# A fused decay attention and ELU layer on one core: one list of pieces in place of a plan that is worked out

## The chip, the core and the metric

One of the eight cores of a Trainium2 chip runs the whole kernel. The metric is the time of one execution in microseconds, the median of the runs shown.

## The reference

Attention with a decay per head runs over 4 batches, 8 heads, 768 positions and 64 columns a head. Its result, seen as 3072 tokens of 512 columns, goes through a layer of two matrices with an ELU between them. The reference goes in blocks of 64 positions; the arithmetic is this:

```python
intra = np.einsum('bhic,bhjc->bhij', qb, kb) * Dmask[None]      # Dmask = lam**(i-j) for i >= j
intra = np.einsum('bhij,bhjd->bhid', intra, vb)
inter = np.einsum('bhid,bhde->bhie', qb * lam_pow[None], kv_state)
out[:, :, sl] = intra + inter
kv_state = lam_block[None, :, None, None] * kv_state + np.einsum('bhsd,bhse->bhde', kb * rev_pow, vb)
...
x = out.transpose(0, 2, 1, 3).reshape(3072, 512)
h = x @ w_in                                                     # 512 x 2048
g = np.where(h > 0.0, h, np.exp(np.minimum(h, 0.0)) - 1.0)
return g @ w_out                                                 # 2048 x 512
```

## The kernel before

The work is cut into 24 blocks of 128 positions, all 8 heads together. Block g belongs to batch g % 4 and to place g // 4 in its sequence, so a block needs the state that block g - 4 left. Both kernels name the steps of a block by letters:

- L: GpSimd issues the loads of q, k and v, which turn float32 into float16 on the way. The first four blocks are loaded alone (128 KB as float16), the others in pairs (256 KB). q of block 0 comes as float32 through SP (`raw_q`) and is cast on DVE. The weights come through the same GpSimd queue in eight slices each, `wi16_0` to `wi16_7` and `wo16_0` to `wo16_7` (wi0, wo0 and so on below, 256 KB each).
- T: q and k are transposed, for blocks 0 to 7 by eight TensorE transposes (`att_T_pe`, L273) with an evacuation of q on DVE (L280, which also scales it by `qs`) and one of k on ACT (L281), for blocks 8 to 23 by two DMA transposes on SP's queue (`att_T_dma`, L258).
- S: the scores, eight matmuls into two PSUM banks (L292); two DVE instructions multiply them by the decay mask (`pp`, L308).
- P: the masked scores times v, and from block 4 on the state times q (L328, L334). One evacuation makes the block's columns of x, `xt` (ACT L349 up to block 7, DVE L351 after).
- U: the block's own part of the state (L387 for one block, L396 for a pair). It reads `kd`, the decayed k that GpSimd makes (L164), and is added on DVE (L408) to the old state that GpSimd has decayed (`stt`, L368, called M).
- the first product of the layer (L468): one piece fills one PSUM bank `psH` of two. For blocks 0 to 3 a piece is four column tiles of one block, 16 matmuls of 128 columns; from block 4 on it is two column tiles of a pair, 8 matmuls of 256 columns. Then ACT makes the exponential (`e`, L474) and the relu (L475), and DVE joins them into `g` (L447), called G in what follows. The piece is named 1:0:0 before and A0:0 after (first block, number).
- the second product (L489): four matmuls of 512 columns into the block's bank `psM`, four such pieces for a block. It is named 2:0:0 before and B0:0 after. Piece j reads wo slices 2j and 2j+1. After the last piece ACT copies the bank out (L515) and SP stores 256 KB. The last 128 columns of block 23 are made by 16 small matmuls at the end (L501).

Each engine runs its instructions in the order in which the program lists them. Before, that order comes from three sources. `POOL_ORDER` is GpSimd's own list up to the loads of block 10. `OPEN` is a list by hand, up to the second product of block 6. After it a loop puts one first product of a pair after another and between them what `AT` says (loads 18 pieces ahead, the DMA transposes 13 ahead, S 8 ahead, P and U together 4 ahead), with one second product after each first one. DVE's work of S, P and U is not put down where TensorE's is: it goes into the list `late`, of which `flush` takes one entry after each G. A store is issued when the next output is ready (`emit_stores(1)`). `BANKS` gives the PSUM banks: T0, T1 and T2 have one bank for q and one for k, the later T one for both.

```python
        if late:
            late.pop(0)()
...
        prog.append(f"1:{g}:{j}")
        prog += extra.pop(u, [])
        n = 2
        while m2 and need[m2[0]] <= u - 2 and n and len(m2) - (len(m1) - 1 - x) > LAGU:
            prog.append("2:%d:%d" % m2.pop(0))
            n -= 1
```

Of the kernel before, what the change touches and what calls it, by code (L numbers as in the profile page):

```python
# [11 lines left out]
ALU = mybir.AluOpType  # L12


@with_exitstack
def kernel(
# [11 lines left out]
    nc = tc.nc  # L28
# [5 lines left out]
    DFF = moe_w_in.shape[1]  # L34
    NFT = DFF // 128
# [3 lines left out]
    NJ = NFT // FB  # L39
    GPE = 8  # L40
    LAST = NG - 1
    CUT = 384
    GSIZE = {**{g: 1 for g in range(4)}, **{g: 2 for g in range(4, NG, 2)}}
    GFIRST = {g0 + i: g0 for g0, n in GSIZE.items() for i in range(n)}
    WI = [2] * 8
    WO = [2] * 8
    POOL_ORDER = (
        "k0 k1 iota q1 k2 v1 i0 v0 q2 i1 v2 i2 o0 i3 d0 q3 o1 i4 k3 i5 o2 o3 v3 d1 m4 d2 d3 i7 "
        "o4 o5 i6 o7 k4 o6 q4 m5 k6 v4 q6 k10 q10 d5 d4 d6 m6 v6 k8 q8 v8 d7 m7 v10"
    )  # L50
    RAW = "q0"
    FIRST = "q0:0 c0 c1 c2"
    OPEN = (
# [7 lines left out]
    )  # L61
    LAGU = 7
    AT = {"L": -18, "W": -13, "T": -9, "S": -8, "B": -4}
    BANKS = (
        "S0=M0,M1 S1=C,D S2=D,M1 S3=D,B P0=M1 P1=B P2=B P3=D U0=M0 U1=D U2=A U3=M1 T0=M1,C "
        "T1=D,A T2=A,D T3=D T4=M0 T5=A T6=M1 T7=D M2=C M3=M0"
    )
    TAGS = {w: t.replace(",", " ") for w, t in (x.split("=") for x in BANKS.split())}

# [4 lines left out]
    asb = ctx.enter_context(tc.tile_pool(name="asb", bufs=1))  # L74
    msb = ctx.enter_context(tc.tile_pool(name="msb", bufs=1))
    ps = ctx.enter_context(tc.tile_pool(name="ps", bufs=1, space=bass.MemoryType.PSUM))

    lam_b = cpool.tile([128, H], FP32, name="lam_b")
    nc.sync.dma_start(out=lam_b[:], in_=lam.unsqueeze(0).broadcast_to([128, H]))

    GROUPS = [(0, 1), (1, 1), (2, 1), (3, 1)] + [(i, 2) for i in range(4, NG, 2)]
    size_of = dict(GROUPS)
    group_of = {g + i: (g, i) for g, n in GROUPS for i in range(n)}
    st = [
        [cpool.tile([128, NHP, 128], FP16, name=f"st{b}_{i}") for i in range(2)]
        for b in range(B)
    ]
    qg, kg, vg = {}, {}, {}  # L90

    def emit_load(w, g0):
        n = size_of[g0]
        c, b = divmod(g0, B)
        x = {"q": q, "k": k, "v": v}[w]
        src = x[b : b + n, :, c * L : (c + 1) * L].rearrange("b h p d -> p (b h) d")
        t = asb.tile([128, n, H, 64], FP16, tag=f"{w}n{n}", name=f"{w}n{g0}", bufs=4)
        {"q": qg, "k": kg, "v": vg}[w][g0] = t
        nc.gpsimd.dma_start(out=t[:].rearrange("p b h d -> p (b h) d"), in_=src)  # L99


    raw = {}
    for w in RAW.split():
        x = {"q": q, "k": k}[w[0]]
        g0 = int(w[1:])
        raw[w] = asb.tile([128, H, 64], FP32, name=f"raw_{w}", tag=f"raw_{w}")
        (nc.sync if w[0] == "q" else nc.scalar).dma_start(
            out=raw[w][:], in_=x[g0, :, 0:L].rearrange("h p d -> p h d")
        )
    nc.scalar.preload_act_table_set("natural_log_exp_and_others")  # L110

    def cast_raw(g, w, eng):
        n = f"{w}{g}"
        t = asb.tile([128, 1, H, 64], FP16, tag=f"{w}n1", name=f"{w}n{g}", bufs=4)
        (qg if w == "q" else kg)[g] = t
        if eng == 0:
            nc.vector.tensor_copy(t[:, 0], raw[n][:])  # L117
        else:
            nc.scalar.copy(t[:, 0], raw[n][:])

    def of(tiles, g):
        g0, i = group_of[g]
        return tiles[g0][:, i]

    wi16, wo16, wi_of, wo_of = [], [], {}, {}
    for i, w in enumerate(WI):
        wi16.append(wpool.tile([128, NHP, w * 128], FP16, name=f"wi16_{i}", tag=f"wi16_{i}"))
        for j in range(w):
            wi_of[sum(WI[:i]) + j] = (i, j)
    for i, w in enumerate(WO):  # L130
        wo16.append(wpool.tile([128, w, DM], FP16, name=f"wo16_{i}", tag=f"wo16_{i}"))
        for j in range(w):
            wo_of[sum(WO[:i]) + j] = (i, j)
    assert sum(WI) == NFT and sum(WO) == NFT

    def emit_wi(i):
        f0 = sum(WI[:i]) * 128
        nc.gpsimd.dma_start(  # L138
            out=wi16[i][:],
            in_=moe_w_in[:, f0 : f0 + WI[i] * 128].rearrange("(k p) f -> p k f", p=128),  # L140
        )

    def emit_wo(i):
        f0 = sum(WO[:i]) * 128
        nc.gpsimd.dma_start(
            out=wo16[i][:],
            in_=moe_w_out[f0 : f0 + WO[i] * 128, :].rearrange("(n p) f -> p n f", p=128),
        )

    iota_c = cpool.tile([128, 1], I32, name="iota_c")  # L150
    iota_r = cpool.tile([128, 128], I32, name="iota_r")

    def emit_iota():
        nc.gpsimd.iota(iota_c[:], pattern=[[0, 1]], base=0, channel_multiplier=1)
        nc.gpsimd.iota(iota_r[:], pattern=[[1, 128]], base=0, channel_multiplier=0)

    kds, qkT, Pt, psS, xg = {}, {}, {}, {}, {}

    def att_kd(g):
        if g // B == NCB - 1:  # L160
            return
        kd = asb.tile([128, H, 64], FP16, tag="kd", name=f"kd{g}", bufs=8)
        kds[g] = kd
        nc.gpsimd.tensor_tensor(  # L164
            out=kd[:], in0=of(kg, g),
            in1=ks[:].unsqueeze(2).broadcast_to([128, H, 64]), op=ALU.mult,
        )


    pool_list = POOL_ORDER.split()  # L170

    def emit_pool():
        w = pool_list.pop(0)
        if w == "iota":
# [75 lines left out]
    for g in range(NG):  # L250
        default_tags(g)
# [401 lines left out]
```

## Time and profile before

| what | value |
|---|---|
| median of 3 runs | 217.68 us (217.17 to 222.01) |
| the profiled execution: its span, first to last instruction | 214.8 us |
| what the median has beyond that span | 2.9 us |
| TensorE busy | 199.5 us, 93% |
| DVE, ACT, GpSimd busy | 130.1, 129.0, 96.2 us |
| DMA: moved, mean rate | 24.59 MB, 114 GB/s |
| granted TensorE clock by the profile | 1.00 in every stretch |
| first and last TensorE matmul | 5.58 and 211.6 us |

The profiled execution has no time of its own beside its span; the 2.9 us are what the runs' median lies above it. A line of a timeline gives the start, the length, the engine, the line of the kernel, what is written and read, how many instructions, and in brackets how long the engine was idle before and what ended that. A matmul's length has the pipeline's own part in it, so the distance between two starts tells more than the length.

### The profile page before, as it was taken

What the parts mean: (1) busy time and instruction counts of PE and PEld (TensorE: products, weight loads), DVE (VectorE), ACT (ScalarE), POOL (GpSimd) and SP (SyncE); (2) the same over time, 40 slices, a digit from 0 to 9 for tenths busy, and PEclk for the clock granted to TensorE, in tenths of its full rate; (3) what the DMA queues carried; (4) which work ended last, traced back from release to release, by engine and by line L of the source; (5) the groups of instructions that cost most, each with busy time, mean ns of one, the idle gap of its engine ahead of it and who ended that gap; (6) DMA issues with size and microseconds to landing.
All of it is one profiled execution on the core that took longest, in us unless ns stands there. A gap on an engine that the chain in (4) does not pass through costs nothing.

```text
span 214.8 us, 5118 instructions
## 1 busy us (share of the span) xinstructions
PE 199.5 (93%) x2048; PEld 138.8 (65%) x2048; DVE 130.1 (61%) x223; ACT 129.0 (60%) x245; POOL 96.2 (45%) x115
## 2 busy tenths in 40 slices
PE   0568999999999998999999999999999999999994
PEld 0456677768685675666766766766766766666652
DVE  3836463777837778668558658657657637533321
ACT  4536665884866656665665675575575576577640
POOL 7998890999996419268068069400000000000000
PEclk9999999999999999999999999999999999999999
DMA  8999999999999955989939919999214110110112
GB/s 90 130 171 194 192 171 176 129 165 145 151 163 144 141 132 128 126 95 145 143 74 134 163 63 115 154 184 138 70 53 97 49 52 0 55 49 8 41 52 98
DMA packets 101976, 24.59 MB, mean 114 GB/s; under 512 B 92608, under 2 KB 99008, under 8 KB 101952
## 3 DMA queue, kind: packets, MB, share of 16 engines
q0 software_dynamic: 79760, 13.50, 83.7%
q1 hardware_dynamic: 22192, 10.76, 24.2%
q8 instruction: 16, 0.26, 0.5%
q14 instruction: 8, 0.07, 0.1%
HBM read 27.27 MB, written 6.29 MB: 156 GB/s over the span
## 4 chain that ended last, share of the span: by engine, by line
PE 84%; DMA 7%; POOL 6%; issue 1%; DVE 0%; SPq 0%; ACT 0%; POOLq 0%
PE psM L489 38%; PE psH L468 36%; DMA wo<-in_moe_w_out_dram 4%; DMA kT<-kn 3%; PE psO L328 3%; PE psS L292 3%; PE psO L334 2%; POOL wi L138 1%; POOL kn L99 1%; POOL vn L99 1%; POOL qn L99 1%; PE psT L273 1%; PE psU L396 1%; POOL kd L164 0%; PE psMrest L501 0%
## 5 line engine op out<-in xcount | busy, mean ns | idle before, releaser
L468 PE MATMUL psH<-xt,wi 128*128 128x256 f16 (+1 forms) x896 | 99.8, 259 | 1.5 <-DVE g L447 0.8
L447 DVE SCALAR_TENSOR_TENSOR g<-e,psH 128x512 f16<-128x512 f32 x96 | 65.8, 686 | 56.3 <-ACT psH L475 55.3
L474 ACT ACTIVATE e<-psH 128x512 f32<-128x512 f32 x96 | 57.3, 597 | 65.7 <-PE psH L468 62.5
L489 PE MATMUL psM<-wo,g 128*128 128x512 f16 (+1 forms) x384 | 95.4, 377 | 0.2 <-DMA wo<-in_moe_w_out_dram 0.2
L468 PEld LDWEIGHTS <-wi 128*128 128x128 f16 x896 | 77.9, 99 | 26.5 <-DVE g L447 2.0
L475 ACT ACTIVATE psH<-psH 128x512 f32<-128x512 f32 x96 | 57.0, 594 | 0.0
L489 PEld LDWEIGHTS <-g 128*128 128x128 f16 x384 | 36.0, 98 | 28.5 <-issue 0.5
L308 DVE TENSOR_TENSOR pp<-psS,mask 128x512 f16<-128x512 f32 x48 | 31.0, 685 | 5.3 <-PE psS L292 5.3
L164 POOL TENSOR_TENSOR kd<-kn,ks 128x512 f16<-128x512 f16 x20 | 20.7, 1039 | 18.4 <-DMA kn<-in_k_dram 17.4
L368 POOL TENSOR_TENSOR stt<-st,upp 64x256 f32<-64x256 f16 x32 | 19.5, 608 | 19.8 <-DVE st L408 13.7
L99 POOL DMA_DIRECT2D kn<-in_k_dram x14 | 15.5, 1104 | 0.8 <-POOLq L637 0.8
L99 POOL DMA_DIRECT2D vn<-in_v_dram x14 | 15.5, 1108 | 0.6 <-DMA wi<-in_moe_w_in_dram 0.6
L515 ACT COPY osb<-psM 128x512 f32<-128x512 f32 x23 | 13.5, 591 | 2.8 <-PE psM L489 2.8
L328 PE MATMUL psO<-pp,vn 128*64 128x128 f16 x192 | 12.4, 230 | 2.6 <-DMA vn<-in_v_dram 2.4
L99 POOL DMA_DIRECT2D qn<-in_q_dram x13 | 14.8, 1137 | 0.0
L408 DVE TENSOR_TENSOR st<-stt,psU 64x256 f16<-64x256 f32 x32 | 13.3, 417 | 1.2 <-PE psU L396 0.5
L328 PEld LDWEIGHTS <-vn 128*64 128x64 f16 x192 | 10.1, 114 | 5.8 <-issue 2.9
L351 DVE TENSOR_TENSOR xt<-psO,qs 128x512 f16<-128x512 f32 x16 | 11.0, 688 | 4.1 <-PE psO L334 4.1
L273 PE MATMUL psT<-ident,qn 128*128 128x128 f16 x32 | 3.8, 252 | 7.0 <-DVE qn L117 5.6
L334 PE MATMUL psO<-qT,st 128*64 128x128 f16 x160 | 10.0, 219 | 0.0
L292 PE MATMUL psS<-qT,kT 64*128 64x128 f16 x192 | 8.7, 228 | 0.7 <-DMA kT<-kn 0.6
L334 PEld LDWEIGHTS <-st 128*64 128x64 f16 x160 | 8.9, 110 | 0.0
(41 smaller groups left out, 67.3 us busy)
## 6 DMA issues: line engine op xcount, KB each, us to landing
out_dram<-osb SPq DMA_DIRECT2D x23, 256.0 KB, 2.4
kn<-in_k_dram POOLq DMA_DIRECT2D x10, 256.0 KB, 8.1
qn<-in_q_dram POOLq DMA_DIRECT2D x10, 256.0 KB, 6.7
vn<-in_v_dram POOLq DMA_DIRECT2D x10, 256.0 KB, 8.4
wi<-in_moe_w_in_dram POOLq DMA_DIRECT2D x8, 256.0 KB, 7.3
wo<-in_moe_w_out_dram POOLq DMA_DIRECT2D x8, 256.0 KB, 8.1
kn<-in_k_dram POOLq DMA_DIRECT2D x4, 128.0 KB, 4.5
vn<-in_v_dram POOLq DMA_DIRECT2D x4, 128.0 KB, 6.2
```

Of the source, the lines that this page charges most:

```text
L99: nc.gpsimd.dma_start(out=t[:].rearrange("p b h d -> p (b h) d"), in_=src)
L164: nc.gpsimd.tensor_tensor(out=kd[:], in0=of(kg, g), in1=ks[:].unsqueeze(2).broadcast_to([128, H, 64]), op=ALU.mult,)
L292: nc.tensor.matmul(psS[g][hh][:, hp, :], lhsT=kt[r, hp, :], rhs=qt[r, hp, :], start=True, stop=True,)
L308: nc.vector.tensor_tensor(out=P[:], in0=pts[hh][:], in1=mask[:, hh::2, :], op=ALU.mult)
L328: nc.tensor.matmul(po[r, hp, :], lhsT=vt[:, 2 * hp + hh, :], rhs=Pt[(g, hh)][:, hp, :], start=True, stop=(cb == 0), skip_group_check=True,)
L334: nc.tensor.matmul(po[r, hp, :], lhsT=st[b][cb % 2][:, hp, r], rhs=qt[:, hp, :], start=False, stop=True, skip_group_check=True,)
L368: nc.gpsimd.tensor_tensor(out=tmp[r], in0=old[r, :, r], in1=upp[r].unsqueeze(2).broadcast_to([64, NHP, 64]), op=ALU.mult,)
L447: nc.vector.scalar_tensor_tensor(out=g[:].rearrange("p f c t -> p (f c t)"), in0=e[:], scalar=-1.0, in1=r[:], op0=ALU.add, op1=ALU.min,)
L468: nc.tensor.matmul(pH[:, f * n * 128 : (f + 1) * n * 128], lhsT=wi16[i][:, kk, w * 128 : (w + 1) * 128], rhs=xg[g0][:, kk, :], start=(kk = ...
L474: nc.scalar.activation(e[:], pH[:], AF.Exp)
L475: nc.scalar.activation(pH[:], pH[:], AF.Relu)
L489: nc.tensor.matmul(psM[g][:, cols], lhsT=gts[(g, j * FB + f)], rhs=wo16[i][:, w, cols], start=first and f == 0, stop=end and f == FB - 1, ...
```

## The change

The three sources of order are replaced by one list, `PROGRAM`, of 881 words. Each word is a piece of work for one engine, and the words of one engine are its instructions in order. A word like `Tq0@D` says the piece, its block and its PSUM bank. Pieces that went together are separate words now: the transposes of q (`Tq`) and of k (`Tk`) for blocks 0 to 2, their evacuations (`tq`, `tk`), the two halves of the masking (`s0.0`, `s0.1`) and of the state's update (`u`), the exponential, relu and G of a first product (`x`, `r`, `m`), the evacuations of x (`p`) and of the output (`o`), the DMA transposes of q and k (`Dq`, `Dk`), and the stores (`st`). H and C are the float32 load of q0 and its cast, `kd` and M are GpSimd's as before, and `z` zeroes a state. T3 to T7 still put q and k into one bank. The instructions of each piece, and how many there are, stay as they were; what they write and the sizes of the buffers too.

In the order: GpSimd's first load is wi1, ahead of its iotas and of k0; wo0 and wo1 come ahead of wi2. U is a piece of its own among P's, first and second products no longer take turns one by one, second products of two blocks are mixed, loads come in an order other than that of their use (v18 and k22 ahead of v10), and the DMA transposes of q and k are single pieces with the stores of earlier outputs between them.

```diff
-    POOL_ORDER = (
-        "k0 k1 iota q1 k2 v1 i0 v0 q2 i1 v2 i2 o0 i3 d0 q3 o1 i4 k3 i5 o2 o3 v3 d1 m4 d2 d3 i7 "
...
-    OPEN = (
-        "z1 z0 z3 Z1 Z2 Z0 z2 T0 T1 S0 S1 P0 P1 T2 1:0:0 S2 1:1:0 P2 U0 M 1:2:0 1:0:1 2:0:0 "
...
-    AT = {"L": -18, "W": -13, "T": -9, "S": -8, "B": -4}
...
+BUFS = {'qn1': 4, 'kn1': 4, 'vn1': 4, 'qn2': 4, 'kn2': 4, 'vn2': 4, 'qT': 5, 'kT': 5, 'pp': 6, 'kd': 8, 'stt': 8, 'xt1': 4, 'xt2': 2, 'xt4': 2, 'e': 3, 'g': 40, 'osb512': 4}
+ON = {'z0.0', 'z2.0', 'z1.0', 'o23', 'z3.0'}
+PROGRAM = (
+    "lam Hq0 wi1 iota Lk0 Lk1 Lq1 Lq2 row pos0 tab Lv1 Lk2 Lv0 wi0 wo0 ln Lv2 wo1 wi2 wi3 pos1 "
+    "pos2 ks kd0 Lk3 llp qs Cq0 z2.0 kd2 kd1 Lq3 wi4 wi5 wo3 wo2 wi7 z0.0 dn wi6 kd3 Lv3 idn "
+    "Tq0@D tq0 cau Tk0@M0 tk0 S0@M1,D Tk1@B Tq1@A tk1 up msk s0.1 s0.0 tq1 S1@B,M1 Tk2@A s1.1 "
+    "Tq2@M0 tk2 s1.0 P0@C p0 P1@B p1 tq2 S2@D,A s2.1 z1.1 wo4 z2.1 A0:0 x0:0 s2.0 r0:0 A1:0 m0:0 "
+    "U2@A U1@D P2@M0 u1.0 x1:0 r1:0 u2.0 m1:0 U0@B p2 u1.1 B0:0@M1 z0.1 A2:0 x2:0 u2.1 r2:0 u0.0 "
+    "m2:0 A1:1 x1:1 r1:1 m1:1 wo5 wo7 B1:0@M0 A2:1 x2:1 r2:1 u0.1 T3@A A0:1 x0:1 tq3 r0:1 B2:0@C "
+    "tk3 m2:1 wo6 A0:2 m0:1 S3@A,D x0:2 r0:2 A2:2 x2:2 r2:2 B1:1 Lq4 Lk4 z3.1 m0:2 Lk6 s3.0 A1:2 "
+    "m2:2 s3.1 x1:2 z1.0 r1:2 Lq6 Lv4 B2:1 kd5 Lq8 Lk8 m1:2 A2:3 P3@A x2:3 U3@D r2:3 B0:1 A1:3 p3 "
+    "x1:3 m2:3 r1:3 A3:2 m1:3 B0:2 B2:2 x3:2 r3:2 A0:3 x0:3 r0:3 u3.1 m3:2 u3.0 m0:3 B1:2 B1:3 "
+    "A3:0 x3:0 o1 B0:3 r3:0 o0 T4@D T5@A tk5 Lv8 tq4 m3:0 tk4 tq5 B2:3 A3:1 S4@M0,B M4 Lk10 "
+    "S5@A,M1 Lq10 M5 s4.0 s5.1 s4.1 x3:1 A3:3 o2 x3:3 s5.0 kd7 r3:3 T6@D B3:0@M0 P4@C P5@B p4 p5 "
+    "m3:3 B3:3 A4:0 r3:1 Lv6 tk6 m3:1 tq6 Dq8 Dq9 Dk9 x4:0 r4:0 T7@B A4:1 kd6 x4:1 m4:0 B3:2 r4:1 "
+    "tk7 A4:3 m4:1 kd9 Lq12 B3:1 tq7 x4:3 r4:3 o3 m4:3 A4:2 S6@M1,B S7@C,A B5:0@M0 M6 A4:5 s7.1 "
+    "x4:2 r4:2 m4:2 A4:4 s7.0 s6.0 s6.1 Dk8 Dq11 P7@C kd4 x4:5 r4:5 m4:5 x4:4 U4_5@A M7 P6@B "
+    "U6_7@D r4:4 z3.0 A4:7 m4:4 p6 p7 B4:0@M1 x4:7 r4:7 kd8 u7.1 u4.0 u7.0 A6:1 m4:7 u4.1 u6.0 "
+    "u6.1 B5:1 A4:6 B5:2 x6:1 r6:1 m6:1 u5.1 x4:6 r4:6 m4:6 u5.0 Lv12 Lv18 A6:7 B4:2 Lq18 kd10 M9 "
+    "x6:7 M8 A6:0 S8@D,A S9@B,C Lk22 Lv16 Lq14 r6:7 x6:0 m6:7 Dq10 A6:3 s9.1 Dq12 st3 r6:0 m6:0 "
+    "s9.0 Dk11 B4:3 s8.1 x6:3 r6:3 m6:3 s8.0 Dk10 A6:4 x6:4 r6:4 B4:1 m6:4 A6:5 U8_9@D u8.0 P9@C "
+    "u8.1 P8@A x6:5 r6:5 kd11 M10 M11 A6:6 m6:5 u9.0 o4 p8 p9 x6:6 r6:6 m6:6 B6:0@M1 u9.1 A6:2 "
+    "B5:3 A8:0 x6:2 r6:2 S11@D,A x8:0 m6:2 r8:0 S10@C,B Dq13 m8:0 st2 o5 s11.0 B6:1 s10.0 A8:3 "
+    "x8:3 r8:3 Lk12 Dk13 st1 m8:3 B7:0@M0 A8:1 x8:1 B6:2 r8:1 Dk12 M13 Lv10 kd12 st5 m8:1 s10.1 "
+    "s11.1 Lk16 B7:1 A8:7 A8:6 x8:7 r8:7 x8:6 Lk14 U10_11@D P10@A P11@C m8:7 r8:6 m8:6 B6:3 p10 "
+    "A8:4 x8:4 A8:5 r8:4 u11.1 B7:3 p11 x8:5 r8:5 m8:4 m8:5 u10.1 B7:2 o7 A10:2 o6 S12@C,M0 "
+    "S13@B,A x10:2 r10:2 s12.1 A10:1 s12.0 m10:2 B9:0@M0 B9:2 x10:1 r10:1 M12 kd15 kd13 kd16 Lk18 "
+    "st6 Dk14 A8:2 s13.1 m10:1 x8:2 r8:2 s13.0 u10.0 A10:3 x10:3 r10:3 u11.0 M15 m8:2 U12_13@C "
+    "u12.0 m10:3 P12@B u13.0 P13@A A10:4 B8:0@M1 Lv14 B9:1 A10:0 B9:3 x10:4 r10:4 p12 u12.1 u13.1 "
+    "x10:0 r10:0 m10:4 A10:7 m10:0 p13 B8:3 x10:7 r10:7 m10:7 A10:5 Lq22 kd14 kd18 Lv22 Dq15 Lq16 "
...
+    "A22:0 x22:0 r22:0 m22:0 st18 st17 st19 B20:1 A22:1 x22:1 r22:1 m22:1 B20:3 o20 B21:3 A22:4 "
+    "x22:4 A22:3 r22:4 x22:3 r22:3 m22:4 B21:1 B22:0@M1 o21 st21 A22:2 st20 st15 m22:3 A22:5 "
+    "x22:5 B23:0@M0 B23:3 r22:5 B22:3 m22:5 B23:2 B22:2 x22:2 r22:2 m22:2 B22:1 o22 B23:1 R@B "
+    "st22 o23 st23 oR stR "
+)
...
+    def transpose(ws, g, banks):
+        pt = bank(banks[0], [128, len(ws), NHP, 128], FP16, f"psT{ws}{g}")
+        for i, w in enumerate(ws):
+            psT[w, g] = pt[:, i]
+            for hp in range(NHP):
+                nc.tensor.transpose(
+                    pt[:, i, hp, :], in_=of(w, g)[:, 2 * hp : 2 * hp + 2, :], identity=ident16[:]
+                )
...
+    def evacuate_t(w, g):
+        t = tr[w, g] = buf(f"{w}T", [128, NHP, 128], FP16, f"{w}T{g}")
+        src = psT.pop((w, g))
+        if w == "q":
+            nc.vector.tensor_tensor(out=t[:], in0=src, in1=qs[:], op=ALU.mult)
+        elif f"tk{g}" in ON:
+            nc.vector.tensor_copy(t[:], src)
+        else:
+            nc.scalar.copy(out=t[:], in_=src)
...
+    def transpose_dma(w, g):
+        t = tr[w, g] = buf(f"{w}T", [128, NHP, 128], FP16, f"{w}T{g}")
+        nc.sync.dma_start_transpose(out=t[:], in_=of(w, g).rearrange("p h d -> p (h d)"))
...
+    def zero_state(b, i):
+        (nc.scalar.memzero(st[b][i][:]) if f"z{b}.{i}" in ON else nc.vector.memset(st[b][i][:], 0.0))
...
+    def store(g, cols):
+        c, b = divmod(g, B)
+        t0 = b * S + c * L
+        nc.sync.dma_start(out=out[t0 : t0 + 128, cols], in_=osb.pop((g, cols.start))[:])
...
+    for word in words:
+        name, _, banks = word.partition("@")
+        banks = banks.split(",")
+        done.add(name)
+        kind = name.rstrip("0123456789.:_")
+        a = [int(x) for x in name[len(kind) :].replace(".", " ").replace(":", " ").replace("_", " ").split()]
+        if name in simple:
+            simple[name](None)
...
+        elif kind in ("T", "Tq", "Tk"):
+            transpose(kind[1:] or "qk", *a, banks)
+        elif kind in ("tq", "tk"):
+            evacuate_t(kind[1], *a)
+        elif kind in ("Dq", "Dk"):
+            transpose_dma(kind[1], *a)
...
```

More of the change, by code (lines that the diff above doesn't have):

```diff
@@ L102 @@
[L102 to L119, printed above, removed]
@@ L134 @@
[L134 to L150, printed above, removed]
@@ new lines, with buf @@
+    wi16 = [
+        wpool.tile([128, NHP, 256], FP16, name=f"wi16_{i}", tag=f"wi16_{i}")
+        for i in range(NFT // 2)
+    ]
+    wo16 = [
+        wpool.tile([128, 2, DM], FP16, name=f"wo16_{i}", tag=f"wo16_{i}")
+        for i in range(NFT // 2)
+    ]
+    R = [slice(0, 64), slice(64, 128)]
+    nat, raw, tr, psT, psS, pp, psO, xg = {}, {}, {}, {}, {}, {}, {}, {}
+    kds, stt, psU, psH, es, gts, psM, osb = {}, {}, {}, {}, {}, {}, {}, {}
+    done = set()
+    def buf(tag, shape, dtype, name):
+        return sb.tile(shape, dtype, tag=tag, name=name, bufs=BUFS.get(tag, 1))
@@ L457, in mm1, with update @@
-    def mm1(g0, j):
-        flush()
-        emit_stores(1)
-        n = GSIZE[g0]
-        assert {f"P{g0 + i}" for i in range(n)} <= seen
-        for i in range(n):
-            until(X_done, g0 + i)
-        pH = ps.tile([128, FB * 128], FP32, tag="psH", bufs=2, name=f"psH{g0}_{j}")
+    def update(g, hh):
+        cb, b = divmod(g, B)
+        r = R[hh]
+        assert cb > 1 or f"z{b}.{(cb + 1) % 2}" in done
+        assert cb == 0 or (f"P{g - B}" in done and f"M{g}" in done)
+        new = st[b][(cb + 1) % 2][r, :, r]
+        if cb == 0:
+            nc.vector.tensor_copy(new, psU.pop((g, hh)))
+        else:
+            nc.vector.tensor_tensor(
+                out=new, in0=stt.pop((g, hh))[r], in1=psU.pop((g, hh)), op=ALU.add
+            )
```

625 lines of the change are left out of this document (223 added, 402 removed), and 28 rows, old and new, of tables (OPEN, PROGRAM).

## The prediction

> **What bounds the kernel now.** I read the page first, then the busy time in stretches, then TensorE's timeline, then GpSimd's and the DMA issues with their times to landing. The page:
>
> ```profile
> span 214.8 us, 5118 instructions
> ...
> PE 199.5 (93%) x2048; PEld 138.8 (65%) x2048; DVE 130.1 (61%) x223; ACT 129.0 (60%) x245; POOL 96.2 (45%) x115
> ...
> PE   0568999999999998999999999999999999999994
> ...
> DMA  8999999999999955989939919999214110110112
> ```
>
> TensorE is busy 93% of the span; its only weak slices are the first four and the last. DVE and ACT are at 60%. The DMA engines are at 9 for the first 75 us. Stretches cut at the events used below:
>
> ```profile
> core 0: us, PE busy (x), PEclk, DMA share, GB/s
> 0.00:5.58 5.58, 0.00 (x0) 1.00 0.92 92
> 5.58:14.60 9.02, 5.04 (x56) 1.00 1.81 144
> 14.60:22.64 8.04, 6.89 (x89) 1.00 1.57 191
> 22.64:43.64 21.00, 21.00 (x262) 1.00 1.57 165
> 43.64:90.36 46.72, 45.34 (x539) 1.00 1.55 144
> 90.36:211.63 121.27, 121.27 (x1114) 1.00 0.77 89
> ```
>
> From 90.36 to 211.63 TensorE is never idle, so no order can shorten that part; it can only put waits in. A busy TensorE may still stretch, so I price work by start-to-start distances: a first product 0.89 us in a group of one block (23.07 to 23.96) and 0.87 in a pair, a second product 0.865 (23.96 to 24.82), a block's transposes 0.45, the scores of a pair 0.65 with their lead-in, P and U of a pair 1.37, of one early block 0.35 and 0.23. By 43.64, when T5 and T4 are done, the kernel has run 15 first products, 10 second products, T0 to T5, S0 to S3, P0 to P3 and U0 to U2: 13.4 + 8.7 + 2.7 + 1.3 + 1.4 + 0.7 = 28.1 us of work, so 15.5 us are lost. In 43.64:90.36 the same prices give 44.8 us of work, so 1.9 are lost; two idle times are most of that:
>
> ```profile
> 70.04 0.40 PE L292 MATMUL psS<-qT,kT 64*128 64x128 f16 x8 [0.61 <-DMA kT<-kn]
> ...
> 84.65 1.05 PE L468 MATMUL psH<-xt,wi 128*128 128x256 f16 x8 [0.77 <-DVE g L447]
> ```
>
> All that can be won is in those 17.4 us. What sets the opening is the loads:
>
> ```profile
> 14.60 1.91 PE L468 MATMUL psH<-xt,wi 128*128 128x128 f16 x16
> 16.45 0.61 PE L292 MATMUL psS<-qT,kT 64*128 64x128 f16 x8
> 16.99 1.07 PE L468 MATMUL psH<-xt,wi 128*128 128x128 f16 x16
> ...
> 19.75 2.23 PE L468 MATMUL psH<-xt,wi 128*128 128x128 f16 x32 [0.60 <-ACT xt L349]
> ...
> 22.64 0.59 PE L489 MATMUL psM<-wo,g 128*128 128x512 f16 x2 [0.23 <-DMA wo<-in_moe_w_out_dram]
> ```
>
> The first product starts at 14.6 (wi0 issued 6.10, landed 11.9; wi1 issued 8.58, landed 14.9), and the first second product finishes only after wo1, issued at 14.51, lands 8.1 us later at 22.6. GpSimd's queue holds up to eight loads in flight: an issue waits for the load eight before it.
>
> ```profile
> 18.66 0.71 POOL L145 DMA_DIRECT2D wo<-in_moe_w_out_dram  x1 [0.33 <-DMA wo<-in_moe_w_out_dram]
> 20.00 0.88 POOL L99 DMA_DIRECT2D vn<-in_v_dram  x1 [0.62 <-DMA wi<-in_moe_w_in_dram]
> ```
>
> Landings follow one another: issue plus time to landing gives 0.85 us after the one before for a 128 KB q, k or v, 1.35 for wi, 1.28 for wo, 1.68 for a 256 KB q, k or v; the first lands 4.44 us after its issue.
>
> **The change, part by part.** *No work is added or removed.* The matmuls, the eight blocks whose transposes TensorE makes, the 32 DMA transposes and every evacuation stay; TensorE's sum stays. T0, T1 and T2 had two banks for q and k already; what is new is that q and k are separate pieces, each evacuated when its own half is done. That alone I price at 0: T0's q half waits for ident, now behind the cast of q0 on DVE (5.8 instead of 5.58), and S0 waits for k0 anyway. The zeroing of st on ACT and DVE (0.40 and 0.27 us each) moves behind other opening work; DVE idles 2.3 us before qT2, which hides it.
>
> *The loads in front.* I place issues and landings by the distances above and the rule of eight. wi1 is issued at 1.25 and lands near 6.2 (4.44, plus 0.5 for its size; bounds 4.4 and 5.1, the shortest of a wi). k0 is now issued at 2.3, not 1.25, and lands at 7.05 instead of 5.70. Then k1 7.9, q1 8.75, v1 10.45, k2 11.3, v0 12.15 (before 12.7), wi0 13.5, wo0 14.8, v2 15.7, wo1 16.95 (before 22.6), wi2 18.3, wi3 19.65, k3 20.5, q3 21.5, wi5 24.3, wo2 26.8, wi6 29.5, v3 30.4, wo6 35.5, q4 37.2, k4 38.9, k6 40.5, q6 42.2, v4 43.9. GpSimd's own queue: 14 issues before kd0 instead of 13, so kd0 starts at 13.3, k3's issue 14.3, kd2 ends 16.2, kd1 17.25, and q3 and wi4 go out behind them.
>
> *TensorE's opening by those times.* S1 at 10.9 (qT1 stands behind pp0 on DVE), P0 12.2 (v0), S2 13.5, A0:0 13.8 at the half rate that the rows show there (16 matmuls in 1.7 us), A1:0 15.5, U2 17.0, U1 17.3 (kd1; this wait of some 0.3 us is new, and P2, U0 and the second products are behind it), U0 done 18.0, B0:0 18.0 instead of 21.8 to 23.1, A2:0 18.9, A1:1 19.8 (wi3), A2:1 21.5, T3 22.4, A0:2 24.6, B1:1 26.8 (wo2), A2:3 29.5 (wi6), P3 30.4 (v3), then no load is late until T4 (k4 38.9); T5 ends at 40.65. By then 14 first and 11 second products and U3 are done, as much work as before plus 0.2. So the opening saves 43.64 - 40.65 + 0.2 = 3.2 us. This leans on loads without a gap; before, v1 landed 0.75 later than its turn and wo1 0.75, so the saving is 1.5 (both again, both in the way) to 3.2; I take 2.6.
>
> *The middle, to T = 90.* The 1.9 us lost before go, since S9's kT and G8's order are other ones; new waits come. k6, v4 and v6 are needed at 43.9, 45.3 and 56.0 by the run of TensorE's work. v4 has 1.4 us to spare. v6 is issued at 49.4, behind kd7, and its turn is 54.0; but from 45.7 on the four DMA transposes of blocks 8 and 9 run beside the loads (before: from 57.9). There q12, k12 and v12, beside four transposes and three stores, came 3.4 us late in all, 0.5 each. So v6 lands at 56 to 57.4, and P7, U4_5 and P6 wait 0 to 1.4, I take 0.8; for q6, v4 and kd4, which have a microsecond or less, 0.5 (0 to 1.5). The middle gains 1.9 - 1.3 = 0.6.
>
> *From 90 on* nothing can be won. First products no longer alternate with second ones one by one: a psH buffer is free 2.25 + 0.69 + 0.06 = 3.0 us after its first product starts (86.39 to g at 88.64, its 0.69, and 84.59 to 84.65). Counting the work between a first product and the one two behind it, the list never goes under 3.03, and a second product never stands less than 3.03 behind the first products that it reads. That fits by 0.03 to 0.3 in some eight places, so a late instruction on ACT or DVE costs there at once: 0 to 2.5, taken 0.6. v10 (issued near 77, behind the state decay of block 13, needed at 83.7; loads took 4.7 to 8.4) and Dk12 (behind k12's landing on SP's queue, needed at 90.3) have about 1.2 us each: in the same 0.6. Stores go out late (st0 behind st7, st4 after 110), but an output buffer is asked for only after one of the four is stored. The tail is the same: B23, R, a copy and a store.
>
> **Sum.** 2.6 + 0.6 - 0.6 = 2.6 us less. The profiled execution spans 214.8; the median of the runs is 217.68, 2.9 us more around it. So 217.7 - 2.6 = **215.1 us**, a span near 212.2.
>
> *A rule that speaks against the change.* The Trainium skill (DMA: Bandwidth & Descriptors, section Queues, rings and completion order) says that a DMA engine takes turns, packet by packet, between the queues that have work. By it the transposes now placed beside k8 to v6 could halve the loads' pace. The trace bears half of this out: k14 landed 3.33 us behind q14 beside transposes, twice 1.68, but q12's group paid 0.5 per transpose or store. The second rival goes by it.
>
> **Rivals.**
> 1. *No wait comes in* (0.26): loads run without a gap and the tight places hold. 3.2 + 1.9 = 5.1 less: 212.6, the floor. For it: each distance was at least 3.0. Against: eight loads within 1.5 us of need.
> 2. *Transposes and loads halve each other* (0.15). Place: v6 before P7. If the five loads k8, v8, k10, q10 and v6 take 3.33 each from 45.6, v6 lands at 62.3 and TensorE waits 6.3 us at P7; with 1.7 at v10 that is 8.0: 217.7 - 5.1 + 8.0 = 220.6, slower than before. It decides from v6 at 61 on, where the wait eats the 5.1. For it: k14's row. Against: q12, k12, v12.
> 3. *The opening is bound by bytes, whatever their order* (0.19). The same 27 loads stand in front of q4; if gaps leave k4 and v4 as late as before (38.5 and 46.5), T5 ends at 43 and P4 waits 1.2: the opening saves 0.6, the middle 0, later waits 0.1: 217.2. For it: DMA at 9 there. Against: q4's turn comes 4 us earlier.
>
> **Chances.** Forecast 0.40 with its own range 213.3 to 216.5. A bound of 2% (4.35 us) is about what a measurement of this kernel can tell from no change. Under 213.3 are most of rival 1 and a little of the forecast: 0.27. Over 222.0 is the upper part of rival 2 only, with more waits at S12 and S14: 0.12. Within: 0.61. The range, 212.3 to 219.8, takes in rivals 1 and 3 and the lower half of rival 2.
>
> **What would show it.** First second product done by 19 (before 23.1); T5 done at 40 to 42; a wait of P on v near 56 under 1.5 us; TensorE idle under 1.5 us after 90; loads' tail (q4) landing near 37 to 39. Wrong: q4 after 41, a P7 wait over 3, or ACT and DVE waits repeated before psH in every pair.

## The result, and the profile after

| what | before | after |
|---|---|---|
| median of 20 runs each, side by side | 217.21 us (215.76 to 222.01) | 215.69 us (213.95 to 218.03) |
| span of the profiled execution | 214.8 us | 213.2 us |
| TensorE busy | 199.5 us | 199.2 us |
| first second product (B0:0) starts | 21.82 us | 18.26 us |
| last TensorE matmul | 211.6 us | 210.1 us |

The ratio of the times is 0.9924 with a 95% interval of 0.9902 to 0.9946: 1.5 us less, where 2.6 less was forecast. That is under 2%, yet 1 lies outside the interval, so the runs tell apart less than the 2% that the prediction allowed for. The ratio is taken over the fast executions only; two slow ones of the changed kernel (217.79 and 218.03) and those of the kernel before are in the medians but not in it.

The page of the changed kernel:

```profile
span 213.2 us, 5052 instructions
PE 199.2 (93%) x2048; PEld 138.5 (65%) x2048; DVE 129.6 (61%) x223; ACT 127.9 (60%) x245; POOL 96.6 (45%) x115
PE   0599989999999999999989999999999999999994
DMA  5999999999999999969997999146110000021042
```

The busy sums are those of before. TensorE's second slice is 5 in both, the third and fourth went from 6 and 8 to 9 and 9: the opening is fuller. Now the stretches cut at the same times as before (length, TensorE busy, its matmuls, granted clock, DMA share, rate):

```profile
14.60:22.64 8.04, 7.90 (x103) 1.00 1.70 186
22.64:43.64 21.00, 20.22 (x247) 1.00 1.82 181
43.64:90.36 46.72, 46.20 (x555) 1.00 1.85 148
90.36:211.63 121.27, 118.66 (x1089) 1.00 0.58 86
```

From 14.60 to 22.64 TensorE gets 103 matmuls done instead of 89. But from 22.64 to 43.64, where it never idled before, it now loses 0.78, and after 90.36, where it never idled either, it loses 1.1 besides ending 1.5 earlier. The waits view from 20 us on has all of it (waiting engine and line, what it waited for, total, times, longest):

```profile
PE psS L287 <- DMA qT<-qn: 1.1, 1, 1.1
PE psH L392 <- DMA wi<-in_moe_w_in_dram: 0.8, 1, 0.8
PE psO L304 <- DMA vn<-in_v_dram: 0.3, 1, 0.3
PE psM L422 <- ACT osb L431: 0.2, 1, 0.2
```

In the timeline, the first product, the first second product, and three of these waits:

```profile
14.39 2.85 PE L392 MATMUL psH<-xt,wi 128*128 128x128 f16 x32
...
18.26 1.03 PE L422 MATMUL psM<-wo,g 128*128 128x512 f16 x4
...
31.02 1.07 PE L392 MATMUL psH<-xt,wi 128*128 128x128 f16 x16 [0.78 <-DMA wi<-in_moe_w_in_dram]
...
58.28 0.25 PE L304 MATMUL psO<-pp,vn 128*64 128x128 f16 x2 [0.33 <-DMA vn<-in_v_dram]
...
107.48 0.62 PE L287 MATMUL psS<-qT,kT 64*128 64x128 f16 x16 [1.09 <-DMA qT<-qn]
```

They are A2:3 waiting for wi6, P7 for v6, and S14 for the DMA transpose of q14.

To see where time comes from and goes, I add up TensorE's pieces, in each kernel's own order, at fixed prices close to those of the prediction and ask when each kernel reaches the same sum. The differences, before minus the other, are the lead (us):

| TensorE work done | at, in before | after | after, again | v6, Dq14 and stores moved | the same, again |
|---|---|---|---|---|---|
| 7 us | 22.8 | 2.60 | 1.15 | 1.40 | 2.60 |
| 18 us | 34.2 | 1.28 | 0.78 | 0.64 | 2.21 |
| 28 us (end of the opening) | 44.5 | 1.60 | 1.10 | 0.96 | 2.52 |
| 70 us | 89.8 | 2.79 | 2.52 | 2.90 | 4.47 |
| 88 us | 108.2 | 2.69 | 2.42 | 2.80 | 4.18 |
| 94 us | 114.4 | 1.52 | 1.47 | 2.80 | 4.18 |
| all | 211.4 | 1.51 | 1.46 | 2.79 | 4.17 |

The last three columns are executions of experiments told below. All compare with the one profile of before that there is. The sums run a little under the prediction's, which has 28.1 us of work done at 43.64, where this table reaches 28 at 44.5. Counted by the prediction's prices exactly, the four leads in the first row are 2.23, 0.78, 1.02 and 2.22, and the other rows change by 0.5 at most in the row of 18 us and by 0.1 in those below it.

### The profile page after: what moved, and what is told of

It reads as the page before. It is cut to its first block, busy times and chain, and to the rows that moved or that the text cites. A ratio compares the mean times of both kernels' runs of the same rounds, so it can differ in the third digit from the quotient of the medians.

```text
span 213.2 us, 5052 instructions
## 1 busy us (share of the span) xinstructions
PE 199.2 (93%) x2048; PEld 138.5 (65%) x2048; DVE 129.6 (61%) x223; ACT 127.9 (60%) x245; POOL 96.6 (45%) x115
## 4 chain that ended last, share of the span: by engine, by line
PE 64%; POOL 17%; DMA 15%; issue 1%; ACT 0%; SPq 0%; POOLq 0%
PE psM L422 29%; PE psH L392 28%; DMA kn<-in_k_dram 5%; DMA vn<-in_v_dram 4%; DMA qT<-qn 4%; POOL wi L245 3%; POOL kn L240 3%; POOL wo L251 3%; POOL kd L332 3%; DMA out_dram<-osb 3%; POOL qn L240 3%; PE psO L304 2%; POOL vn L240 2%; PE psO L310 2%; PE psS L287 2%
## 5 line engine op out<-in xcount | busy, mean ns | idle before, releaser
L392 PE MATMUL psH<-xt,wi 128*128 128x256 f16 (+1 forms) x896 | 97.6, 259 | 0.9 <-DMA wi<-in_moe_w_in_dram 0.8
L422 PE MATMUL psM<-wo,g 128*128 128x512 f16 (+1 forms) x384 | 92.7, 377 | 0.2 <-ACT osb L431 0.2
L392 PEld LDWEIGHTS <-wi 128*128 128x128 f16 x896 | 77.5, 99 | 22.8 <-DMA wi<-in_moe_w_in_dram 1.3
L287 PEld LDWEIGHTS <-kT 64*128 64x128 f16 x192 | 5.9, 98 | 5.8 <-issue 3.6
```

Source lines behind the costliest of these rows:

```text
L287: nc.tensor.matmul(psS[g, hh][:, hp, :], lhsT=tr["k", g][r, hp, :], rhs=tr["q", g][r, hp, :], start=True, stop=True,)
L392: nc.tensor.matmul(pH[:, f * n * 128 : (f + 1) * n * 128], lhsT=wi16[i][:, kk, w * 128 : (w + 1) * 128], rhs=xg[g0][:, kk, :], start=(kk = ...
L422: nc.tensor.matmul(psM[g][:, cols], lhsT=gts[g, f], rhs=wo16[i][:, w, cols], start=f == 0, stop=f == NFT - 1, skip_group_check=True,)
```

## The experiments

**Is the late loss only S14, and is it only the place of one transpose?** In the changed kernel Dq14 stands last of seven entries on SP's queue, behind st6 (which waits for o6), three transposes and two stores: issued at 99.89, landed at 107.44.

```diff
- st6 Dk14 ... Dq15 Dk15 st7 st0 Dq14
+ Dk12 Dq14 ... st6 Dk14 ... Dq15 Dk15 st7 st0
```

> One word of the new list moved: the DMA transpose of block 14's q goes right behind that of block 12's k on SP's queue, ahead of five stores and three other transposes. Theory (the list's lead over the old kernel is 2.8 us at the third quarter of the work and 1.1 of it is lost at block 14's scores, which wait for qT14 because SP issues it at 99.9 and it lands 7.6 us later): qT14 lands before 98, the scores start without a wait, and the time falls by 1.0 us (0.7 to 1.2) against the new kernel, about 0.988 of the old one's. Rival (transposes and loads share the DMA engines, so what is freed is paid by the others): kT14, kT15 or v10 come later by as much and the time stays at 0.992 of the old one's, within 0.3 us.

Measured: 214.80 us beside 217.48 of the kernel before, ratio 0.9896 (0.9838 to 0.9953). Dq14 now stands ahead of four stores (the expectation counts five) and three transposes. qT14 was issued at 86.74, landed at 93.45, and S14 waited for nothing. The lead stayed 1.44 from 88 us of work to the end, where the changed kernel lost 1.17 there: in the profile the late loss is this one transpose. The time shows less of it, and its interval overlaps with that of the changed kernel; in this profile v6 landed at 59.48 and P7 waited 1.3.

**Does wi1 as the first load buy anything?**

```diff
- lam Hq0 wi1 iota Lk0 ... Lv0 wi0 wo0
+ lam Hq0 iota Lk0 ... Lv0 wi0 wi1 wo0
```

> One word of the new list moved: wi1 is no longer GpSimd's first load but goes right behind wi0; everything else stands. Theory (the first first product needs wi0 and wi1 together and no byte is saved): k0 lands 1.4 us earlier, S0 starts about 1 us earlier, wi1 lands near 13.7 as the last of the same ten loads, the first first product starts within 0.3 us of 14.4, and the time is within 0.4 us of the new kernel's, 0.991 to 0.994 of the old one's. Rival (the slice in front is what makes the new opening): the first first product starts a wi's turn later, 15.7, and the time rises by 1 us or more, to 0.997 or above.

Measured: 215.23, ratio 0.9900 (0.9849 to 0.9951). k0 landed at 6.03 and S0 started at 7.70; wi0 landed at 13.24, wi1 at 14.57, the first product started at 14.28 instead of 14.39 and the first second product at 18.01. At 28 us of work the lead was 1.60, as in the changed kernel, so its place gives the opening nothing that shows. The total of this profile was worse (S14 waited 1.84 for its transpose, against 1.09), and the intervals of the two times overlap.

**Is it wo0 and wo1, loaded early, that make the opening shorter?** First they go back to where the kernel before has them:

```diff
- wi0 wo0 ln Lv2 wo1 wi2 wi3 ... Lk3 ... Lq3 wi4
+ wi0 ln Lv2 wi2 wo0 wi3 ... Lk3 ... Lq3 wo1 wi4
```

> Two words of the new list moved back to where the old kernel has them: wo0 behind wi2, wo1 behind q3. TensorE's order stays. Theory (the lead of the opening, 2.6 us at 7 us of work, comes from second products that can run at 18 because both slices of w_out are there): wo1 lands near 23.2, the first second product and the two first products behind it wait some 4 to 5 us, of which the wait for wi6 near 31 gives back about 1; the time rises by 3 us (2 to 4.5) against the new kernel, to 1.006 of the old one's (1.002 to 1.013). Rival (the opening is bound by the bytes, so that order within it costs little): TensorE waits for the late weights near 30 anyway, and the rise is under 1 us.

Measured: 218.17, ratio 1.0045 (1.0012 to 1.0078), by the ratios 2.6 us more than the changed kernel, inside the expected range. The first second product, which the list puts ahead of most first products, stands in front of an idle TensorE:

```profile
18.23 0.59 PE L422 MATMUL psM<-wo,g 128*128 128x512 f16 x2 [0.28 <-DMA wo<-in_moe_w_out_dram]
22.55 1.01 PE L422 MATMUL psM<-wo,g 128*128 128x512 f16 x2 [3.72 <-DMA wo<-in_moe_w_out_dram]
23.35 1.91 PE L392 MATMUL psH<-xt,wi 128*128 128x128 f16 x16
```

The last line shows a cost that was not forecast: 16 matmuls took 1.91 us and not 0.9. Behind the wait the granted clock was 0.50 from 22.26 to 25.67. The half second product took 0.80 instead of 0.43 and the two first products behind it 2.90 instead of 1.78, so some 1.5 us of the loss are the clock and not the wait. Ten of the twelve runs have a mean granted clock of 0.991 or 0.992, which is what one such stretch makes of it. The waits for wi6, v6 and o5 of the changed kernel did not come in return, and S14 waited 0.3 only.

So the list needs these two loads early. Does the kernel before gain by the same move?

```diff
-        "k0 k1 iota q1 k2 v1 i0 v0 q2 i1 v2 i2 o0 i3 d0 q3 o1 i4 ...
+        "k0 k1 iota q1 k2 v1 i0 v0 q2 i1 v2 o0 o1 i2 i3 d0 q3 i4 ...
-        "... 1:0:0 S2 1:1:0 P2 U0 M 1:2:0 1:0:1 2:0:0 "
+        "... 1:0:0 S2 1:1:0 P2 U0 M 2:0:0 1:2:0 1:0:1 "
```

> The old kernel with one part of the new order alone: wo0 and wo1 loaded ahead of wi2, and the first second product (2:0:0) placed right behind U0 instead of two first products later. Theory (this is the main part of the opening's lead): the second product runs near 19 in the time in which TensorE waited for xt and for wo1, the work done at 23 us is 1.1 us ahead of the old kernel's, half of that is lost again at later weights and at the wait for block 9's transposed k: 0.7 us less than the old kernel (0.3 to 1.2), a ratio of 0.997. Rival (the lead needs the whole new order): no change, 1.000 within 0.001, or slower because wi2 and wi3 land 2.6 us later.

Measured: 217.35, ratio 1.0010 (0.9967 to 1.0052): no gain, and my theory was wrong. The mechanism worked and the gain was gone three microseconds later:

```profile
18.31 1.04 PE L489 MATMUL psM<-wo,g 128*128 128x512 f16 x4
...
21.89 0.29 PE L468 MATMUL psH<-xt,wi 128*128 128x128 f16 x2 [1.08 <-DMA wi<-in_moe_w_in_dram]
```

The lead at 6 us of work was 1.72. Then wi3, now behind wo0 and wo1 and 2.4 us behind wi2, cost 1.08 of it, and further late weights left 0.15. Here an earlier start only brought TensorE to the next load sooner. So the two early loads are needed for the lead of the whole list, but they don't make it alone. Which of the list's other changes keeps TensorE fed behind them was not taken apart and stays open.

**The three late places mended, and the changed kernel beside it.**

```diff
- kd5 Lq8 Lk8 ... Lk10 ... Lq10 ... kd7 ... Lv6
+ kd5 Lv6 Lq8 Lk8 ... Lk10 ... Lq10 ... kd7
- Dq13 st2 ... Dk13 st1 ... Dk12 ... st6 ... st0 Dq14
+ st2 st1 Dq13 ... Dk13 ... Dk12 Dq14 ... st6 ... st0
```

> The changed kernel with its three late places mended at once: Dq14 right behind Dk12, v6 loaded ahead of q8, st2 and st1 ahead of Dq13. Theory (what the change loses after the opening stands in these three waits: S14 1.1 us, P7 0.3 to 0.7, a second product behind o5 0.2): 1.6 us under the unchanged list run beside it (1.0 to 2.0), v6 landed near 46.5, no wait of TensorE over 0.2 us after 45. Rival (loads and transposes are only pushed onto one another, and the next late one takes the place): under 0.5 us less, with a new wait of 0.5 to 1.5 at S8, S12 or P10.

> The changed kernel itself, beside the others on the same chip. Theory: 0.992 of the kernel before, 1.7 us less; its opening (first and second products up to T5) 1.6 us ahead of before, S14 waiting about 1.1. Rival (a single profile was lucky or unlucky by a us in the landing of wi6 and of qT14): the lead at 43 us or the wait at S14 differs from that by more than 0.5 us in this profile.

Measured on one chip: 213.27 us for the mended version, ratio 0.9826 (0.9790 to 0.9862), and 214.83 for the changed kernel, 0.9890 (0.9860 to 0.9920), with 217.34 for the kernel before. That is 1.56 less by the medians, where 1.6 was expected. In the mended version v6 lands at 47.42, and after 20 us the waits view has one line, 0.3 us of P3 for v3. The table's columns show it: after 88 us of work no lead is lost again. The rival for the changed kernel was half right: its S14 wait came again (0.88), but at 43 us its lead was 1.10 and not 1.60.

**The mended version once more, and with block 3 put off in the opening.**

```diff
- kd0 Lk3 ... kd2 kd1 Lq3 wi4 wi5 wo3 wo2 wi7 ... wi6 kd3 Lv3
+ kd0 ... kd2 kd1 wi4 wi5 wo3 wo2 wi7 ... wi6 Lk3 Lq3 Lv3 ... Lk6 kd3
- A2:1 T3 A0:1 B2:0 A0:2 S3 A2:2 B1:1 A1:2 B2:1 A2:3 P3 U3 B0:1 A1:3 A3:2 B0:2 B2:2 A0:3
+ A2:1 A0:1 B2:0 A0:2 A2:2 B1:1 A1:2 B2:1 A2:3 A1:3 T3 B0:1 A0:3 S3 B0:2 B2:2 P3 U3
```

> The version with the three late places mended once more, beside the one above on its chip. Theory: 0.983 of the kernel before (0.979 to 0.986), no wait of TensorE over 0.35 us after 20 but one on a late load before 33. Rival (its first result was a lucky placing of the loads): 0.987 or more, and a wait over 0.5 us at P7 or S14 again.

> The version with the three late places mended, and in the opening block 3 put off: k3, q3 and v3 are loaded behind all wi and wo0 to wo3, and T3, S3, P3 and U3 stand behind the last first products of blocks 1 and 2. Theory (after 27 us TensorE has eaten what the loads brought, so the order of the bytes is what limits the opening's gain): wi6 lands near 29.2, its wait of 0.8 and the one on v3 go, T5 ends 0.5 to 1.0 earlier, the time is 0.4 to 1.0 us under the same version without it. Rival (the sum of bytes up to q4 limits, and a wait at k3, q3 or wo5 takes the place): within 0.3 us of it, T5 ends where it did.

Measured: 213.20 us, ratio 0.9820 (0.9790 to 0.9850), for the mended version again, so its gain holds. With block 3 put off 214.38, 0.9891 (0.9849 to 0.9934): 1.2 us worse, and the theory fell. wi6 landed at 28.80 and nothing waited for it, but A1:3, now right behind A2:3, waited 0.50 for its psH buffer, that is for a g on DVE. At 28 us of work the lead was 0.42; the weaker profile of the mended version, with v0 late as here, has 0.96, so this wait can account for the 0.5 between them. Whether it is all of the 1.2 us in the times, one profile can't say. That the bytes limit the opening this run neither shows nor refutes, since what stopped TensorE was a buffer and not a load. The second profile of the mended version is the best of all, with TensorE without a wait from 22.64 on:

```profile
22.64:43.64 21.00, 21.00 (x269) 1.00 1.82 181
43.64:90.36 46.72, 46.72 (x543) 1.00 1.95 149
```

**What does a DMA transpose cost the loads beside it?** The store of block 3, which waits for o3, goes ahead of all DMA transposes, so that k8 to v6 have the loads' path alone.

```diff
- Dq8 Dq9 Dk9 ... Dk8 Dq11 ... Dq10 Dq12 st3
+ st3 Dq8 Dq9 Dk9 ... Dk8 Dq11 ... Dq10 Dq12
```

> The changed kernel with the store of block 3 ahead of all DMA transposes on SP's queue, so that they start after o3 (near 54.6) and not at 46.6. From 45 to 54 the loads k8, v8, k10, q10 and v6 then run alone. Theory (each transpose beside the loads costs them about 0.5 us): v6 lands at 55 to 56.5 instead of 58.2, P7 does not wait. Rival by turns packet by packet (a transpose takes half of the loads' pace): v6 lands at 53.5 or earlier, at its undisturbed distance of 1.68 per load. Third (transposes cost loads nothing, the issue of v6 at 50.4 and its queue set it): 57.5 to 58.5 as now. In all cases S8 and S9 at 70 may wait for the later transposes, 0 to 2 us.

Only the part up to 60 us is read. The run paid later: Dq14 landed at 109.11, S14 waited 3.44 for it, and behind that wait the granted clock was 0.50 from 110.13 to 113.55. Its two times, 218.37 and 214.20, say nothing of the change. v6, issued at 50.37 in the changed kernel and at 50.31 here, has these times from issue to landing, in this order:

```profile
DMA to landing us min/median/max: 7.9/7.9/7.9
```

```profile
DMA to landing us min/median/max: 4.7/4.7/4.7
```

It landed at 55.03 instead of 58.23, and P7 did not wait. 3.2 us for the four transposes are 0.8 each, not 0.5 (a fifth, Dq11, was issued at 55.33 and is not counted). By single loads: k8 and v8 kept their 1.7 us in both kernels; k10, q10 and v6 came 2.88, 2.51 and 2.97 us behind one another with transposes in flight, and 1.66, 1.68 and 1.88 without. The second rival had 3.33 for each of the five loads, 8.3 us in all; my price made it 2.0 in all. The pace of the three loads in flight beside transposes is nearer to the rival's, the sum of 3.2 is nearer to mine. The Trainium skill (DMA: Bandwidth & Descriptors, section Queues, rings and completion order) lets an engine take turns between queues, and this trace, with 2.5 to 3.0 us in place of 1.7 to 1.9, agrees with it in the main.

**Do the two banks for q and k matter?** Blocks 0, 1 and 2 with one bank each:

```diff
- Tq0@D tq0 cau Tk0@M0 tk0 ... Tk1@B Tq1@A tk1 ... Tk2@A s1.1 Tq2@M0 tk2
+ T0@D tq0 cau tk0 ... T1@A tk1 ... T2@A s1.1 tk2
```

> The changed kernel with q and k of blocks 0, 1 and 2 transposed into one PSUM bank each, as T3 to T7 do, eight matmuls in a row, then both evacuations. Theory (the two banks are worth nothing, loads set the opening): S0 at most 0.6 us later (it now waits for both halves), S1 at 11.2 as before, the first product at 14.4, time within 0.3 us of the unchanged list. Rival (separate banks let S0 and S1 go earlier and the opening's chain of scores and first products rests on it): first product 0.6 to 1.2 us later, time 0.5 to 1.2 us more.

Measured: 215.25, ratio 0.9917 (0.9881 to 0.9952), beside 0.9890 (0.9860 to 0.9920) with two. S0 started at 8.77 and not 8.08, S1 at 12.07 and not 11.20, the first product at 15.60 and not 14.81, but v0 was also 0.3 later in this execution. The intervals overlap; a few tenths for the banks can be neither shown nor excluded. Since the kernel before had the two banks for these blocks already, it is no part of the difference to it.

**The pace of the first products.** In all profiles the distance of two early 128-column matmuls is 107 ns and then 56, but the fall comes at 16.3 us in the changed kernel, near 19 in its second profile and at 14.8 in the best one of the mended version. The same 32 matmuls, A0:0 and A1:0, in the best one and then in the changed kernel's second profile:

```profile
14.40 2.14 PE L392 MATMUL psH<-xt,wi 128*128 128x128 f16 x32
```

```profile
14.81 3.60 PE L392 MATMUL psH<-xt,wi 128*128 128x128 f16 x32
```

So ten transposes of ident, read by nobody, fill the idle time ahead of S1, in the mended version and in the changed kernel:

```diff
- tq1 S1@B,M1
+ tq1 F0@H S1@B,M1      # F: ten transposes of ident into a bank of psH
```

> The version with the three late places mended, and ten further transposes of ident on TensorE in its idle time ahead of S1 (10.1 to 11.2), into a bank nobody reads: no other engine and no load is touched. Theory (in the profiles so far the distance of two early matmuls fell from 107 to 56 ns between 14.9 and 18.2 us, because it takes some 3.4 us without a gap in TensorE, seen in windows of that length whose start differs from execution to execution; the gap ahead of S1 breaks the first one): it falls between 12 and 15.4 here, the two first products from A0:0 on take 2.0 us and not 2.7 to 3.4; where the loads are not late the second product starts at 18.3 as before, since kd1 ends at 17.3; the time is 0 to 0.6 us under the version without them (0.982 of the kernel before), with less spread. Rival (the pace has nothing to do with what TensorE did before): it falls at 15 to 18.2 as in the others, and the ten cost 0 to 0.5 us.

> The changed kernel with the same ten transposes of ident ahead of S1. Theory: the distance of two matmuls falls to 56 ns between 12 and 15.4 us, A0:0 and A1:0 take 2.0 us; the time is 0 to 0.6 us under the changed kernel (0.989 to 0.992 of the kernel before). Rival: it falls between 15 and 18.2 as in the eleven profiles without them, time the same or up to 0.5 us more.

Measured: 213.34, ratio 0.9845 (0.9792 to 0.9897), and 214.90, 0.9893 (0.9850 to 0.9936): no change of the time by either. The distance fell to 56 ns at 14.7, in the expected stretch, and at 11.7, a little ahead of it, and both are earlier than in any of the twelve profiles without the ten. But 14.7 is only 0.1 ahead of the earliest of these (14.8), so it tells nothing; the theory rests on the 11.7 of one profile. (The latest fall without the ten is that of the changed kernel's second profile, near 19, and not the 18.2 of the two expectations.) Then each met something else. In the mended version U1 waited 0.60 for kd1, which GpSimd ends at 17.3, so the first second product started at 18.28 again. In the changed kernel wi0 was late, TensorE idled 1.05 ahead of A0:0, and the clock went back to the half:

```profile
11.70:14.20 2.50, 1.89 (x35) 1.00 1.38 181
14.20:15.20 1.00, 0.00 (x0) 0.94 1.75 170
15.20:18.60 3.40, 3.36 (x33) 0.51 1.45 195
18.60:22.00 3.40, 3.40 (x53) 1.00 1.95 176
```

The number behind the count of matmuls is the granted clock: 0.51 for 3.4 us, and A0:0 and A1:0 took 3.3 us from start to U2.

## Why the prediction was right or wrong

**The total** came out 1.5 less instead of 2.6 less. The time itself, 215.69 against 215.1, misses by only 0.6, and part of that is luck: the median of the first three runs, 217.68, was 0.5 above the 217.21 of twenty, so the forecast started too high. In all runs on record a time lies 1.7 to 1.9 us above its own span; the 2.9 of the prediction compared a quick execution with a slower median. Beside the mended version the changed kernel gained more, 2.5 us by the medians (ratio 0.9890), so the gain is known to about a microsecond only. By the leads of the profiles three terms make the 1.5:

| term | predicted | changed kernel | other profiles |
|---|---|---|---|
| opening, to 28 us of work | 2.6 (1.5 to 3.2) | 1.6 | 1.0 to 2.5 |
| from there to 88 us | 0.6 | 1.1 | 1.3 (again), 0.1 (Dq14 moved, P7 waiting 1.3), 1.7 to 1.8 with v6 early |
| after 88 us | -0.6 (0 to -2.5) | -1.2 | -1.0 (again), 0 with Dq14 early |

The right-hand column counts the executions with the changed kernel's opening: the changed kernel again, the one with Dq14 moved, and the mended version twice and with the ten transposes. It leaves out the run with st3 moved, whose lead at 28 us of work was 1.5, and the changed kernel with the ten transposes, where the clock went back and the lead was 0.3.

**The opening: right mechanism, mis-sized term.** The landings were forecast well as long as nothing was late: v0 12.15 against 12.57, wi0 13.5 against 13.65, wo1 16.95 against 17.42, wi3 19.65 against 20.10, wi7 28.15 (one distance of 1.35 behind wo2) against 28.43. B0:0 was forecast at 18.0 and started at 18.26. The term failed at wi6: it landed 2.54 us behind wi7 instead of 1.35, at 30.97 instead of 29.5, and A2:3 waited 0.78. From there on every landing was about a microsecond late (q4 38.13 against 37.2, v4 44.83 against 43.9), and T5 ended at 42.25 instead of 40.65. The prediction named this ("this leans on loads without a gap") and then took 2.6, nearer to no gap than to two. In all fourteen profiles one to four loads of the first 45 us land 0.35 to 1.7 us behind their turn, other ones each time, and whenever TensorE has no other work that time is lost. Among the profiles only the best comes to 2.5, and there wi3 was 0.5 and v3 0.45 late. A fair term was 1.5, the mean of these six. The late loads are not the only thing that differs: the matmuls' distance falls from 107 to 56 ns at 16.3 us in the changed kernel, near 19 in its second profile and at 14.8 in the best one, and A0:0 and A1:0 took 2.7, 3.4 and 2.0 us in them. No run keeps the two apart.

**Priced at nothing:** wi1 in front, rightly as far as its experiment can tell; the two banks, which both kernels have; and st's zeroing, which nothing waits for. The wait of U on kd1, priced at 0.3, was almost nothing here: U2 started at 17.09 and U1 at 17.36, as forecast (17.0 and 17.3), but U2's matmuls ran until then. Where the first products were done earlier it came: 0.60 in the best profile.

**The middle: two errors that offset each other.** The wait of S9 on kT and the one on G8 went, as forecast. v6 landed at 58.23, later than the 56 to 57.4 of the prediction: its turn without transposes was 55.0 instead of 54.0, and the four transposes cost 0.8 each and not 0.5 (0 to 1.4 us of a wait had been allowed for). But TensorE came to P7 at 57.95 and not at 56, for the most part since the opening had given less, so the wait was 0.33 and not 0.8. The 0.5 taken for q6, v4 and kd4 did not come; instead B7:0 waited 0.19 for o5, which stood 0.8 us behind the store st2 on its output buffer. The prediction said of stores that a buffer is asked for only after one of the four is stored: st2 was issued at 74.90, behind Dq13, and landed at 80.45.

**After 90 us: the wrong place.** The prediction put its 0.6 on distances of 3.03 between first products, on v10 and on Dk12. No such wait came: TensorE has no wait on g there, v10 landed at 84.56 and kT12 at 90.11, both in time. What cost 1.09 was Dq14, whose place behind st6, three transposes and two stores was not followed, though the prediction had S14 among the places for trouble. A queue's last entry is late by the sum of what is ahead of it, and by its own landing: 2.4 us for a transpose with little beside it (kT13 in the best profile), 7.55 here.

**The rivals.** *No wait comes in* (212.6) is not what the kernel did, but it is near what it can do: with four words moved it takes 213.2 to 213.3, and its best profile leads by 4.17 of the 5.1. *Halving* was nearly right about the pace while transposes are in flight (2.5 to 3.0 us, not 3.33) and wrong about the price: only the three loads behind the first transposes were slowed, and v6 came at 58.2, not 62.3. *Bound by bytes* (217.2) holds in part: early wo0 and wo1 alone gave the kernel before nothing, and where a load near 30 us came late TensorE waited for it (wi6 here, v3 in the first profile of the mended version). The best profile, without a wait from 22.64 on, speaks against the rest of it.

**The signs to look for:** first second product done by 19 (19.13, just missed), T5 done at 40 to 42 (42.25, just missed), P7's wait under 1.5 (0.33), q4 at 37 to 39 (38.13), TensorE idle under 1.5 after 90 (1.1). The two that were missed both belong to the opening, the term that was priced too well.

## What to carry to other kernels

When an opening lives on one stream of loads, price it with one load a microsecond late where TensorE has no other work: a chain of landings without a gap is the best case, and an earlier start of one piece only moves the wait to the next load. When an order is written by hand, follow each in-order DMA queue to its last entry and add up what is ahead of it, stores that wait for a result above all: here one transpose at the end of SP's queue took back 1.1 of 2.7 us, and moving it with one load and two stores brought the time to 0.982 (0.979 to 0.985) of the kernel before. A gain that disappears should be looked for in the lead at equal work, not in busy shares, which hardly moved here.

## What the runs showed of the hardware that was not expected

The pace of the first matmuls differs from execution to execution of one kernel: 107 ns apart until 14.8 to 19 us, 56 after, with the granted clock at 1.00 in the profile's rows all the while. The same holds for the kernel before (107 ns until 17.0). So the distance of matmuls tells the pace there, and the clock row does not.

Later on the clock row does show it. In three profiles it fell to the half for 3.4 us. Within each of them the changes of the clock in the trace lie 3.41 us or a multiple of it apart: up at 11.68, down at 15.09, up at 18.50 (changed kernel with the ten transposes); up at 15.43, down at 22.26, up at 25.67 (wo0 and wo1 moved back); up at 17.97, down at 110.13, up at 113.55 (st3 moved). In the 3.41 us before the fall TensorE was busy 1.9 us, not at all, and 1.0 us. The length of an idle time alone doesn't decide: an idle time of 1.05 us stands ahead of the first of these falls, while one of 1.09 (S14 in the changed kernel) and one of 1.84 (S14 with wi1 moved) brought none, though in the stretch around the latter TensorE was busy 1.7 of 3.41 us by the profile. How idle a stretch has to be is open. The Trainium skill (TensorE: Matmul & The Clock Gate, section Part 1: The HAM clock gate) tells of a gate that looks at windows of some 3.4 us which run on whatever the kernel does, and fits the spread and the distances; the fall after a stretch in which TensorE was busy for 1.9 us is not in its rule of one idle window, and there the run decides.

The loads that come late in the opening are not the same ones from profile to profile. Many of those after 20 us (wi6 at 30.97 in the changed kernel, wi3 at 21.84 in the kernel before with wo0 and wo1 early) land 1 to 3 us after one of the 16 KB instruction fetches that the trace has on one DMA engine for about 1 us (at 28.95 and 19.67); others, v0 at 13.2 to 13.6 among them, have none near. No run tested it, and the cause is open.
